# Attention and a GELU feed-forward on one core: how the first GEMM of a batch is opened

## The chip, the cores and the metric

The kernel runs on one core of a Trainium2 chip. The time is the device time of one execution in microseconds; the median of three runs stands for a kernel. A separate execution was recorded by the hardware profiler; its rows name engines: PE is TensorE (matmuls), DVE is VectorE, ACT is ScalarE, POOL is GpSimd, SP is the engine that issues most DMAs.

## The reference

Eight batches of eight heads, 576 tokens, head dimension 64; then a feed-forward with 512 inputs, 2048 hidden units and 512 outputs, on all 4608 tokens.

```python
scores = scale * np.matmul(q, k.transpose(0, 1, 3, 2))
log_f = np.log(np.clip(f, 0.0001, 1.0))
cum = np.cumsum(log_f, axis=-1)
decay = cum[:, :, :, None] - cum[:, :, None, :]
scores = np.where(causal, -1000000000.0, scores + decay)
attn = softmax(scores)
x = (attn @ v), heads side by side, (B * S, H * D)
h = x @ w_in
out = gelu(h) @ w_out          # exact GELU, with erf
```

## The kernel before

**Batches and stages.** The loop at the end runs over the eight batches. For batches 2 to 7 `attention(b)` (line 828) does the attention of batch b and opens its first GEMM; the loop behind it finishes that GEMM. The second GEMM of batch b - 1 is not a stage of its own: `gemm2_rows` (line 489) is a generator, one step at each `yield`, and `take(fill, n)` runs n steps of it wherever the attention of batch b has room. Batches 3 to 7 use `PLAN` (line 472) and the counts in `FILL` (line 825); batch 2 uses other plans.

**The order is written by hand.** Each engine executes its instructions in the order in which the program emits them, and so does each DMA queue. Waits between engines are semaphores that the framework places from the reads and writes of the tiles.

**Scores.** The heads are taken in four pairs, i = 0 to 3. For each pair `scores` (line 299) makes four tiles, t = 0 to 3: matmuls on 64 rows into a tile of two PSUM banks (tag `s`, two such tiles in all), an exp on ScalarE from PSUM into SBUF, and for the tiles on the diagonal a mask on GpSimd. After tile t of pair i come `FILL[i][t]` steps of the second GEMM. The third tile of any row needs the buffer of the tile two before it, so it waits for that tile's exp.

**The second GEMM's steps.** A row tile of 128 tokens (ts = 0 to 3) has 16 steps, one for each block of 128 hidden units. A step "r" is two matmuls on 64 rows each, into two banks; a step "n" is one matmul on 128 rows into the first bank. After the last "r" VectorE copies the second bank to `ot`, and after the last step it adds the first (line 533) and SP stores the tile. Row tiles 0 and 2 hold the two banks of tag `o`, 1 and 3 those of tag `m`. In row tiles 0 to 2 all 16 steps are "r", and the two banks change their parts at the end, so that the bank allocated first is copied first. For row tile 3 the copy is put off (line 521) until `put_off.pop()()` (line 867), after AV.

**AV.** For a pair, `av(i, n)` makes the two heads' products: `attend` (line 343) is 15 matmuls of 65 columns into one bank of tag `o`, `normalize` (line 358) a reciprocal and a multiply on VectorE from that bank into `x`. n steps of the second GEMM stand between the two heads. Then `x_dma` (line 388) transposes the pair's part of `x` into `xT` by a DMA that SP issues. There are two `o` banks, so a head waits for the normalisation of the head two before it, and the first two heads wait for what empties row tile 2's banks.

**The first GEMM.** `gemm1(c, ffb, kts, ps, act)` (line 400) computes block ffb of 128 hidden units (16 blocks), with four matmuls of 512 columns; number kt needs the x transpose of pair kt. `gelu` on ScalarE takes the bank to SBUF. Before, batches 3 to 7 open four blocks in the four `s` banks: kt 0 and 1 of blocks 0 and 1; kt 2 of the same; kt 0 to 2 of blocks 2 and 3; kt 3 of all four; then the four gelus; then block 4 in an `m` bank. The loop goes on with block 5; blocks 6 and 7 lie in `o` banks (`spare`, line 416), the others alternate between the two `m` banks.

**Beside it.** While the first GEMM runs, VectorE unpacks q and k of the next batch (`untangle`, line 260), GpSimd weighs its v (`weigh_v`, line 283), copies the last 64 tokens into `tails` (`x_tail`, line 394) and issues the loads of q and k two batches ahead. SP issues the transposes of q and k, the loads of v, the stores of the output, and the x transposes, all in one queue. The 64 last tokens of every batch go through both GEMMs after batch 7.

Of the kernel before, what the change touches and what calls it, by code (L numbers as in the profile page):

```python
# [9 lines left out]
FP32 = mybir.dt.float32  # L10
# [5 lines left out]
P = 128  # L16
# [3 lines left out]
HP = 4  # L20
# [34 lines left out]
def kernel(  # L55
# [35 lines left out]
    s_psum = ctx.enter_context(tc.tile_pool(name="s_psum", bufs=2, space=PSUM))  # L91
# [153 lines left out]
    def transpose_dma(b, h0, h1):  # L245

        if b >= B:
            return
        if b not in tq_of:
            tq_of[b] = [  # L250
                tq_pool.tile([P, H, JT // 2, PT], BF16, tag="t" + n, name=f"t{n}{b}")
                for n in "qk"
            ]
        for src, dst in zip(qk_of[b], tq_of[b]):
            nc.sync.dma_start_transpose(
                dst[:, h0:h1].rearrange("d h j p -> d (h j) p"),
                src[:, h0:h1].rearrange("p h c -> p (h c)"),
            )
# [84 lines left out]
    def attend(b, i, h, ms, pool=o_psum, tag="o"):  # L343
        if (b, i, h) not in o_of:
            o_of[b, i, h] = pool.tile([P, NBLK, D + 1], FP32, tag=tag, name="o")
        o = o_of[b, i, h]
        for m in ms:
            for n in range(m + 1):
                t, c = where(n, m)
                nc.tensor.matmul(  # L350
                    o[:, m, :],
                    e_of[b, i, t][:, h, c : c + P],
                    vw_of[b][:, 2 * i + h, n, :],
                    start=(n == 0),
                    stop=(n == m),
                )

    def normalize(b, i, h):
        if (b, i) not in x_of:
            x_of[b, i] = x_pool.tile([P, NBLK, 2, D], BF16, tag="x", name="x")  # L360
        o = o_of[b, i, h]
        r = x_pool.tile([P, NBLK], FP32, tag="r", name="r")
        nc.vector.reciprocal(r, o[:, :, D])  # L363
        nc.vector.tensor_tensor(  # L364
            x_of[b, i][:, :, h, :],
            o[:, :, 0:D],
            r.unsqueeze(2).to_broadcast([P, NBLK, D]),
            Alu.mult,
        )

    def xT(b):
        if b not in xT_of:
            xT_of[b] = xT_pool.tile([P, n_dm, XC], BF16, tag="xT", name="xT")
        return xT_of[b]
# [13 lines left out]
    def x_dma(b, i):  # L388
        nc.sync.dma_start_transpose(
            xT(b)[:, i, :].rearrange("d (m p) -> d m p", p=P),  # L390
            x_of[b, i].rearrange("p m h d -> p (m h d)"),
        )
# [7 lines left out]
    def gemm1(c, ffb, kts=range(4), ps=None, act=True):  # L400
        src = xT(c) if c < B else tails
        if ps is None:
            ps = m_psum.tile([P, TC], FP32, tag="m", name="ps1")
        for kt in kts:
            nc.tensor.matmul(  # L405
                ps,
                w_in_sb[:, kt, ffb * P : (ffb + 1) * P],
                src[:, kt, 0:TC],
                start=(kt == 0),
                stop=(kt == n_dm - 1),  # L410
            )
        if n_dm - 1 in kts and act:
            gelu(c, ffb, ps)
        return ps

    def spare():
        return o_psum.tile([P, TC], FP32, tag="o", name="ps1")

    def gelu(c, ffb, ps):
        if c not in g_of:  # L420
            g_of[c] = [
                g_pool.tile([P, TC], BF16, tag=f"g{n}", name=f"g{n}")
                for n in range(n_ff)
            ]
        nc.scalar.activation(g_of[c][ffb], ps, Act.Gelu)  # L425
# [9 lines left out]
    def gemm2(c):  # L435
# [37 lines left out]
        (0, "o", 16 * "r"),  # L473
        (1, "m", 16 * "r"),
        (2, "o", 16 * "r"),
        (3, "m", 4 * "r" + 12 * "n"),
    ]

    PLAN_0 = [(2, "o", 16 * "r"), (3, "m", 14 * "r" + 2 * "n")]
# [105 lines left out]
    def gemm2_third():  # L585
        yield from gemm2_second(0)
        yield from gemm2_rows(0, PLAN_0)
        yield from gemm2_rows(1, PLAN_1)

    def take(gen, n):  # L590
        for _ in range(n):
            if next(gen, "end") == "end":
                return
# [228 lines left out]

    FILL = [[7, 4, 3, 3], [3, 3, 3, 3], [3, 3, 3, 3], [3, 3, 3, 2]]
    FILL_2 = [[8, 8, 8, 8], [8, 8, 4, 4], [4, 4, 4, 4], [4, 4, 4, 4]]

    def attention(b):


        fill = gemm2_third() if b == 2 else gemm2_rows(b - 1, PLAN)
        counts = FILL_2 if b == 2 else FILL

        def av(i, n=0):
            for h in range(2):
                attend(b, i, h, (0, 1, 2, 3, 4))
                normalize(b, i, h)
                if h == 0:
                    take(fill, n)
            x_dma(b, i)  # L840

        for i in range(HP):
            for t in range(4):
                scores(b, i, t)
                take(fill, counts[i][t])
                if t == 1 and b == 2 and i > 0:
                    av(i - 1)
                    if i == 1:
                        load_v(3)
                if b == 2 and (i, t) == (0, 3):  # L850
                    weigh_v(b, 2)
                    weigh_v(b, 3)
                if b > 2 and i == 0 and t == 1:
                    load_v(b + 1)
                if b > 2 and t == 0 and i < 2:
                    transpose_dma(b + 1, 4 * i, 4 * i + 4)
                if b == 2 and t == 1 and i == 1:
                    transpose_dma(3, 0, 4)
        if b == 2:
            take(fill, 4)  # L860
            av(HP - 1)
        else:
            av(0)
            for i in range(1, HP):
                take(fill, 1)
                av(i, 1)
            put_off.pop()()
        take(fill, 4)
        if b == 2:
            transpose_dma(3, 4, 8)  # L870
        take(fill, 999)

        if b == 2:
            pss = [gemm1(b, ffb, (0, 1)) for ffb in range(2)]
            pss += [spare(), spare()]
        else:
            pss = []
            for _ in range(2):
                wide = s_psum.tile([P, 2, 512], FP32, tag="s", name="ps1")
                pss += [wide[:, 0, :], wide[:, 1, :]]  # L880
            for ffb in range(2):
                gemm1(b, ffb, (0, 1), pss[ffb])
        for ffb in range(2):
            gemm1(b, ffb, (2,), pss[ffb])
        for ffb in (2, 3):
            gemm1(b, ffb, (0, 1, 2), pss[ffb])
        for ffb in range(4):
            gemm1(b, ffb, (3,), pss[ffb], b == 2)
        for ffb in range(0 if b == 2 else 4):
            gelu(b, ffb, pss[ffb])  # L890
        if b == 2:
            more = s_psum.tile([P, 2, 512], FP32, tag="s", name="ps1")
            gemm1(b, 4, ps=more[:, 0, :])
        else:
            gemm1(b, 4)
        if b + 1 < B:
            untangle(b + 1, 0)
            weigh_v(b + 1, 0)
        x_tail(b)
# [64 lines left out]
    for b in range(B):  # L964
        if b == 0:
            first_attention()
        elif b == 1:
            second_attention()
        else:
            attention(b)  # L970
        for ffb in range(4 if b < 2 else 5, n_ff):
            if b == 0 and ffb in HELD:
                continue
            aside = ffb in ((7, 8) if b == 2 else (6, 7)) if b > 1 else b == 1 and ffb % 4 < 2
            gemm1(b, ffb, ps=spare() if aside else None)
            if b == 1 and ffb % 2 == 0:
                at = HELD[(ffb - 4) // 2]
                gelu(0, at, h_of[at])
            if b == 0:
                if ffb == 4:  # L980
                    attend_tail()
                if ffb == 5:
                    tail_0()
                if ffb == 7:
                    weigh_v(1, 0)
                    load_w_out(0)
                    weigh_v(1, 1)
                    load_w_out(1)
                    load_qk_tokens(2)
                if ffb == 8:  # L990
                    transposes_first(1, 0, o_psum, "o")
            elif b + 1 < B:
                first, gap = (5, 3) if b == 1 else (1, 4)
                at, late = divmod(ffb - first, gap)
                if late == 0:
                    untangle(b + 1, at)
                if late == gap - 2 and (b > 1 or at < 2):
                    weigh_v(b + 1, at)
                if ffb == (9 if b == 1 else 14):
                    load_qk_tokens(b + 2)  # L1000
# [34 lines left out]
```

## Time and profile before

| what | value |
|---|---|
| median of 3 runs | 340.0 us (339.42 to 340.82) |
| the profiled execution | 340.29 us |
| its span | 338.6 us, 8109 instructions |
| TensorE busy | 322.1 us (95%) |
| ScalarE busy | 205.6 us (61%) |
| VectorE busy | 189.3 us (56%) |
| granted TensorE clock, batches 3 to 7 | 1.00 |
| batches 3 to 7, first score matmul to the next | 36.1, 36.8, 35.7, 35.9, 36.3 us |

A row of a timeline has its start and length in us, the engine, the line of the kernel, the operation, output and inputs, the tile sizes, a count of instructions that were merged, and in brackets the idle time before it with what ended it. Matmuls are pipelined: the bar of one is longer than the distance between two starts. "64*128" is a matmul on 64 rows, "128*128" on 128. A few per cent of the matmul records are missing. Of a group of merged rows the name is that of the first.

### The profile page before, as it was taken

To read this page: it belongs to the slowest core of one execution; us is meant where nothing else is said; L and a number is where in the kernel's file an instruction comes from. 1 tells how busy PE (TensorE), PEld (TensorE's weight loads), DVE (VectorE), ACT (ScalarE), POOL (GpSimd) and SP (SyncE) were. 2 spreads that over 40 slices of the span, in tenths; PEclk is the share of its full clock that TensorE was granted. 3 is DMA by queue.
4 is the path that set the end of the run, shared out by engine and by line. 5 is a ranking of instruction groups with operands and counts; after the bars stand their busy time and mean duration, and the time that the engine had idled before them with its cause. 6 is when DMAs were issued, how large, how long until landed. Compare 5 with 4: busy or idle time off the path is not lost.

```text
span 338.6 us, 8109 instructions
## 1 busy us (share of the span) xinstructions
PE 322.1 (95%) x3284; PEld 174.3 (51%) x3322; DVE 189.3 (56%) x432; ACT 205.6 (61%) x296; POOL 134.2 (40%) x260
## 2 busy tenths in 40 slices
PE   8999999999999998999989999999999989999995
PEld 4654555445544556446634564456545564444443
DVE  5843765755469538963898259934994280020011
ACT  4986867954707991689347962798088916404600
POOL 8987871076354251715261535434252500000000
PEclk9999999999999999999999999999999999999999
DMA  7999999959989695499929983979500151011012
GB/s 116 202 195 214 214 195 132 211 113 202 204 203 181 124 216 129 83 137 223 161 58 159 215 154 95 138 153 223 110 1 2 64 91 50 0 69 57 0 48 79
DMA packets 94949, 44.19 MB, mean 131 GB/s; under 512 B 74176, under 2 KB 89792, under 8 KB 94912
## 3 DMA queue, kind: packets, MB, share of 16 engines
q1 hardware_dynamic: 77760, 27.16, 41.7%
q0 software_dynamic: 16752, 15.99, 29.8%
q8 instruction: 26, 0.43, 0.6%
q10 hardware_dynamic: 400, 0.52, 0.4%
q14 instruction: 11, 0.09, 0.1%
HBM read 36.85 MB, written 9.44 MB: 137 GB/s over the span
## 4 chain that ended last, share of the span: by engine, by line
PE 79%; DMA 7%; ACT 5%; DVE 3%; POOL 3%; issue 2%; POOLq 0%; ACTq 0%; DVEq 0%
PE ps L405 35%; PE ps L509 20%; PE ps L449 8%; PE o L350 7%; PE s L319 6%; DMA xT<-x 5%; ACT L329 2%; ACT e L329 2%; DVE x L364 2%; DMA v_sb<-in_v_dram 2%; ACT g L425 1%; PE ps L573 1%; DVE r L363 1%; PE ps L549 1%; POOL k L120 1%
## 5 line engine op out<-in xcount | busy, mean ns | idle before, releaser
L425 ACT ACTIVATE g<-ps 128x512 bf16<-128x512 f32 x138 | 78.4, 602 | 92.8 <-remote 47.0
L405 PE MATMUL ps<-xT,w_in_sb 128*128 128x512 bf16 x494 | 112.7, 379 | 4.5 <-DMA xT<-x 3.5
L509 PE MATMUL ps<-w_out_sb,g 64*128 64x512 bf16 (+1 forms) x732 | 106.7, 376 | 0.5 <-issue 0.5
L329 ACT ACTIVATE e<-s 128x896 bf16<-128x896 f32 x112 | 87.8, 836 | 14.2 <-PE s L319 9.8
L405 PEld LDWEIGHTS <-w_in_sb 128*128 128x128 bf16 x576 | 55.2, 97 | 70.8 <-issue 7.3
L331 POOL TENSOR_SCALAR_AFFINE_SELECT e<-e 128x256 bf16<-128x256 bf16 (+1 forms) x135 | 49.1, 384 | 79.4 <-ACT e L329 79.0
L509 PEld LDWEIGHTS <-g 64*128 64x128 bf16 (+1 forms) x746 | 42.5, 94 | 28.7 <-issue 1.3
L288 POOL TENSOR_TENSOR vw<-v_sb,wT 128x640 bf16<-128x640 f32 (+1 forms) x30 | 38.3, 1276 | 38.1 <-PE o L350 17.1
L269 DVE COPY qT<-tq 64x288 bf16<-64x288 bf16 x96 | 45.0, 469 | 3.0 <-DMA tq<-q 1.5
L523 DVE COPY ot<-ps 128x512 f32<-128x512 f32 x20 | 13.8, 692 | 56.6 <-PE ps L509 56.6
L269 DVE COPY kT<-tk 64x288 bf16<-64x288 bf16 x96 | 37.9, 395 | 3.9 <-DMA tk<-k 2.2
L319 PE MATMUL s<-qT,kT 64*128 64x256 bf16 (+1 forms) x336 | 37.8, 275 | 1.9 <-DVE kT L241 0.6
L350 PE MATMUL o<-vw,e 128*128 128x65 bf16 x840 | 34.5, 194 | 2.5 <-DVE r L363 1.5
L350 PEld LDWEIGHTS <-e 128*128 128x128 bf16 x840 | 31.0, 97 | 10.1 <-issue 7.0
L458 DVE COPY ot<-ps 128x512 f32<-128x512 f32 (+2 forms) x9 | 5.7, 632 | 50.5 <-PE ps L449 50.5
L319 PEld LDWEIGHTS <-kT 64*128 64x128 bf16 x336 | 18.1, 94 | 20.9 <-issue 6.0
L364 DVE TENSOR_TENSOR x<-o,r 128x320 bf16<-128x320 f32 x56 | 27.5, 491 | 1.9
L449 PE MATMUL ps<-w_out_sb,g 128*128 128x512 bf16 (+2 forms) x142 | 27.9, 355 | 0.2
L449 PEld LDWEIGHTS <-g 128*128 128x128 bf16 x144 | 13.5, 98 | 14.5
L533 DVE TENSOR_TENSOR ot<-ot,ps 128x512 f32<-128x512 f32 x27 | 18.6, 687 | 2.5
L405 PE MATMUL ps<-tails,w_in_sb 128*128 128x512 bf16 x63 | 14.2, 377 | 0.1
L363 DVE RECIPROCAL r<-o 128x5 f32<-128x5 f32 x56 | 10.7, 191 | 4.9 <-PE o L350 3.0
(90 smaller groups left out, 185.8 us busy)
## 6 DMA issues: line engine op xcount, KB each, us to landing
out_dram<-ot SPq DMA_DIRECT2D x32, 256.0 KB, 2.3
v_sb<-in_v_dram SPq DMA_DIRECT2D x24, 256.0 KB, 4.7
q<-in_q_dram POOLq DMA_DIRECT2D x6, 576.0 KB, 6.4
k<-in_k_dram POOLq DMA_DIRECT2D x6, 576.0 KB, 8.6
v_sb<-in_v_dram POOLq DMA_DIRECT2D x17, 128.0 KB, 5.7
w_in_sb<-in_moe_w_in_dram POOLq DMA_DIRECT2D x4, 512.0 KB, 7.8
w_out_sb<-in_moe_w_out_dram POOLq DMA_DIRECT2D x4, 512.0 KB, 8.1
v_sb<-in_v_dram SPq DMA_DIRECT2D x6, 128.0 KB, 4.7
```

The source lines that it names most:

```text
L269: nc.vector.tensor_copy(rows[:, odd], src[odd * D : (odd + 1) * D, 2 * i + h].rearrange("d j p -> d p j"),)
L288: eng.tensor_tensor(vw(b)[:, hs, n0:n1, 0:D], v_sb[:, hs, n0:n1, :], w.unsqueeze(3).to_broadcast([P, 2, n1 - n0, D]), Alu.mult,)
L319: nc.tensor.matmul(to, *ab, start=half < 0, stop=half == 1 or not masked)
L329: nc.scalar.activation(et[:, :, z:c], st[:, :, z:c], Act.Exp, scale=scale)
L331: nc.gpsimd.affine_select(out=et[:, :, c0 + z : c0 + P], in_=et[:, :, c0 + z : c0 + P], compare_op=Alu.is_ge, fill=0.0, base=z, pattern=[[ ...
L350: nc.tensor.matmul(o[:, m, :], e_of[b, i, t][:, h, c : c + P], vw_of[b][:, 2 * i + h, n, :], start=(n == 0), stop=(n == m),)
L364: nc.vector.tensor_tensor(x_of[b, i][:, :, h, :], o[:, :, 0:D], r.unsqueeze(2).to_broadcast([P, NBLK, D]), Alu.mult,)
L405: nc.tensor.matmul(ps, w_in_sb[:, kt, ffb * P : (ffb + 1) * P], src[:, kt, 0:TC], start=(kt == 0), stop=(kt == n_dm - 1),)
L425: nc.scalar.activation(g_of[c][ffb], ps, Act.Gelu)
L449: nc.tensor.matmul(pss[ts][:, c0:c1], g_of[c][kt][:, ts * P : (ts + 1) * P], w_out_sb[:, kt, c0:c1], start=(kt == 0), stop=(kt == n_ff - 1),)
L509: nc.tensor.matmul(banks[r], g_of[c][kt][rows, ts * P : (ts + 1) * P], w_out_sb[rows, kt, :], start=kt == (steps.index("r") if r else 0), ...
L533: nc.vector.tensor_tensor(ot, ot, bank, Alu.add)
```

## The change

For batches 3 to 7 alone:

- Row tile 3 of the second GEMM has two "r" and fourteen "n" steps, where it had four and twelve.
- The steps between score tiles: eight where there were seven after the first tile, and 3, 2, 3, 0 in the last pair where there were 3, 3, 3, 2. In all 50 where there were 52.
- The steps in AV follow `FILL_AV`, pairs of (steps before the pair, steps between its heads): none in pair 0, then 3 and 1, 2 and 1, 2 and 1. Before, it was none, then 1 and 1 for each. In all 10 where there were 6; the last four steps come after AV, where there were six.
- `gemm1_open` opens six blocks, 0 to 3 in the `s` banks, 4 and 5 in the `o` banks: kt 0 and 1 of all six, kt 2 of all six, then kt 3 and the gelus for block 4, block 5, blocks 0 and 1, blocks 2 and 3.
- The loop leaves block 5 out, since it is done; blocks 8 and 9 lie in `o` banks, where it was 6 and 7. Block 6 is the first in an `m` bank.

```diff
-        (3, "m", 4 * "r" + 12 * "n"),
+        (3, "m", 2 * "r" + 14 * "n"),
...
-    FILL = [[7, 4, 3, 3], [3, 3, 3, 3], [3, 3, 3, 3], [3, 3, 3, 2]]
+    FILL = [[8, 4, 3, 3], [3, 3, 3, 3], [3, 3, 3, 3], [3, 2, 3, 0]]
+    FILL_AV = [(0, 0), (3, 1), (2, 1), (2, 1)]
...
+    def gemm1_open(b):
+        pss = []
+        for _ in range(2):
+            wide = s_psum.tile([P, 2, 512], FP32, tag="s", name="ps1")
+            pss += [wide[:, 0, :], wide[:, 1, :]]
+        pss += [spare(), spare()]
+        for ffb in range(6):
+            gemm1(b, ffb, (0, 1), pss[ffb])
+        for ffb in range(6):
+            gemm1(b, ffb, (2,), pss[ffb])
+        for pair in ((4,), (5,), (0, 1), (2, 3)):
+            for ffb in pair:
+                gemm1(b, ffb, (3,), pss[ffb], False)
+            for ffb in pair:
+                gelu(b, ffb, pss[ffb])
...
-            av(0)
-            for i in range(1, HP):
-                take(fill, 1)
-                av(i, 1)
+            for i, (n0, n1) in enumerate(FILL_AV):
+                take(fill, n0)
+                av(i, n1)
             put_off.pop()()
-        take(fill, 4)
         if b == 2:
+            take(fill, 4)
             transpose_dma(3, 4, 8)
         take(fill, 999)
...
-            gemm1(b, 4)
+            gemm1_open(b)
...
-            aside = ffb in ((7, 8) if b == 2 else (6, 7)) if b > 1 else b == 1 and ffb % 4 < 2
-            gemm1(b, ffb, ps=spare() if aside else None)
+            aside = ffb in ((7, 8) if b == 2 else (8, 9)) if b > 1 else b == 1 and ffb % 4 < 2
+            if b <= 2 or ffb > 5:
+                gemm1(b, ffb, ps=spare() if aside else None)
```

More of the change, by code (lines that the diff above doesn't have):

```diff
@@ L875, in attention @@
             pss += [spare(), spare()]
[L876 to L880, printed above, removed]
-            for ffb in range(2):
[L882 to L891, printed above, removed]
+            for ffb in range(2):
+                gemm1(b, ffb, (2,), pss[ffb])
+            for ffb in (2, 3):
+                gemm1(b, ffb, (0, 1, 2), pss[ffb])
+            for ffb in range(4):
+                gemm1(b, ffb, (3,), pss[ffb])
             more = s_psum.tile([P, 2, 512], FP32, tag="s", name="ps1")
```

## The prediction

> **What bounds the kernel now.** I read the page's busy shares first, then TensorE's waits, then the timeline of one middle batch engine by engine, and laid the other four beside it. TensorE is the bound:
>
> ```profile
> PE 322.1 (95%) x3284; PEld 174.3 (51%) x3322; DVE 189.3 (56%) x432; ACT 205.6 (61%) x296; POOL 134.2 (40%) x260
> ```
>
> The change adds and removes no TensorE work to speak of, so only gaps can move. The list of waits says where they are in batches 3 to 7 (columns: total us, times, longest):
>
> ```profile
> PE ps L405 <- DMA xT<-x: 3.5, 5, 1.3
> PE o L350 <- DVE r L363: 1.5, 5, 0.3
> PE o L350 <- DVE x L364: 1.0, 5, 0.2
> ```
>
> These understate the gaps, since a matmul's bar runs on after the next could have started. I count starts instead. Batch 4 on TensorE, from the last steps between scores to the first GEMM (L405):
>
> ```profile
> 161.59 0.61 PE L509 MATMUL ps<-w_out_sb,g 64*128 64x512 bf16 x4
> 162.13 1.26 PE L350 MATMUL o<-vw,e 128*128 128x65 bf16 x30
> 163.68 0.64 PE L350 MATMUL o<-vw,e 128*128 128x65 bf16 x15 [0.30 <-DVE r L363]
> ...
> 165.22 0.64 PE L350 MATMUL o<-vw,e 128*128 128x65 bf16 x15
> 165.69 0.38 PE L509 MATMUL ps<-w_out_sb,g 128*128 128x512 bf16 x1
> 165.91 0.64 PE L350 MATMUL o<-vw,e 128*128 128x65 bf16 x15
> 166.76 0.63 PE L350 MATMUL o<-vw,e 128*128 128x65 bf16 x15 [0.21 <-DVE x L364]
> ...
> 167.92 1.46 PE L509 MATMUL ps<-w_out_sb,g 128*128 128x512 bf16 x6
> 169.21 1.03 PE L405 MATMUL ps<-xT,w_in_sb 128*128 128x512 bf16 x4
> 171.59 10.73 PE L405 MATMUL ps<-xT,w_in_sb 128*128 128x512 bf16 x48 [1.35 <-DMA xT<-x]
> ```
>
> A full matmul starts every 0.216 us (167.92 to 169.21 is six). A head of AV takes 0.47 (165.22 to 165.69). Two heads and two steps are 1.37, yet heads start 1.54 apart two by two (163.68, 165.22, 166.76): 0.17 of gap each time. From 162.13 to 163.68 stand two heads and one step, 1.16, so 0.39 of gap. AV loses 0.73 per batch. (A step in front of 163.68 and of 166.76 has no record; the program has it.) The first GEMM stops after four matmuls: 169.21 + 4 x 0.216 = 170.08, restart 171.59, 1.51 lost on the third x transpose.
>
> Between the scores there is one more gap:
>
> ```profile
> 149.70 1.03 PE L509 MATMUL ps<-w_out_sb,g 64*128 64x512 bf16 x8
> 150.80 0.37 PE L319 MATMUL s<-qT,kT 64*128 64x448 bf16 x2
> ```
>
> Four steps from 149.70 end at 150.56; the third score tile waits until 150.80 for ScalarE (gelu 147.92, table load, first exp from 149.83, 0.92 long).
>
> **The change, part by part.**
>
> *Two "r" steps become "n".* Twelve half matmuls, six pairs, take 1.46 in a row, so a pair starts every (1.46 - 0.38)/5 = 0.217. Same as a full one: nothing.
>
> *First slot 7 to 8.* The third score tile stays where ScalarE puts it; the eighth step fills 0.22 of the 0.24.
>
> *Fourth score group 3,3,3,2 to 3,2,3,0.* All steps now lie one earlier against the score tiles, so step 48, the last of row tile 2, ends about 0.19 earlier (0.02 is lost to the first exp of that group, which ends just as its buffer is wanted). What step 48 releases matters, because AV's heads need its two banks:
>
> ```profile
> 161.22 0.69 DVE L523 COPY ot<-ps 128x512 f32<-128x512 f32 x1 [3.01 <-PE ps L509]
> 162.01 0.69 DVE L533 TENSOR_TENSOR ot<-ot,ps 128x512 f32<-128x512 f32 x1
> ```
>
> Before, two steps covered this. Now TensorE stands in front of the first two heads: head 1 starts 0.05 after the add, at 162.70 - 0.19 + 0.05 = 162.56.
>
> *Steps inside AV 0,0 / 3,1 / 2,1 / 2,1.* From 162.56: seven heads 3.29 and ten steps 2.16, end 168.01. Two heads with three steps are 1.59, over VectorE's 1.54, so its gaps close. Before, AV ended at 167.92 with 58 steps done; now 168.01 with 60. Gain 2 x 0.216 - 0.09 = 0.34 per batch, 1.7 for five. Ends: 0.15 if step 48 comes no earlier; 0.97 if every gap of AV and scores (0.73 + 0.24) went. I take 0.34, which follows the rows.
>
> *Six blocks opened.* Let E be the end of AV. Before, six steps and four matmuls ran before the third x transpose was wanted (the second already by the second of these four). Now four steps stand in front, then twelve matmuls on the first two transposes, six on the third, six on the fourth. The second is wanted at E + 5 x 0.216, where it was E + 7 x 0.216, the third at 16 and the fourth at 22 matmul times. With E 0.09 later, that is E + 1.17, E + 3.55 and E + 4.84 by the old E. The same transfers in the five batches (E, the start of the row of six steps: 131.90, 167.92, 204.73, 240.37, 276.34): in batch 3 TensorE stopped after one matmul, on the second transfer, until 134.13; in the others after four, until 171.59, 207.23, 243.20, 279.55. Lost before: 0.72, 1.51, 0.34, 0.67, 1.05, in all 4.29. After, with landings where they were: batch 3 134.13 - 133.07 = 1.06; batch 4 0.12; batch 5 0.01; batch 6, whose second transfer is issued at 238.24 and takes 3.6 to land, 0.30; batch 7 nothing (the tails copy behind its fourth transfer starts 281.09, wanted 281.18). In all 1.49: gain 2.8. Ends: 4.3 if no transfer is late; -1.0 if the second is late in all five as in batch 3 (5 x 1.06 = 5.3).
>
> One transfer in each batch is the late one, and it is never the same:
>
> ```profile
> 164.22 6.75 SPq L389 DMA_TRANSPOSE xT<-x  x4
> ```
>
> Undisturbed, an issue takes 1.2 and landing 2.4; in batches 3 to 7 the worst took 4.1, 4.2, 3.4, 3.6, 3.8. Within 2 us after each one's issue starts one packet of the instruction queue (131.87, 168.52, 201.68, 238.94, 276.49). There are 26 of them to some 6,600 TensorE instructions (3284 and 3322), one in 254. At E as many instructions have been issued after the change as before in batch 3, and four fewer per batch after that, so I leave the landings where they are. The Trainium skill, "Runtime: NRT & Kernel Launch", section "Instruction fetch mechanics", says that instructions are refilled in blocks of 16 KB and that crossing a block is mostly hidden. By that rule no transfer would be late for it, and this term would be the 4.3; the trace's coincidence says otherwise, and the sum goes by the trace.
>
> *Gelu order, banks 8 and 9.* With T the first last-k matmul, six come in 1.30, then blocks of 0.863 follow; the next to need a ScalarE release late is block 12 at T + 6.47, on block 10, the eleventh gelu. Before, seven gelus in a row stood thus:
>
> ```profile
> 173.94 3.62 ACT L425 ACTIVATE g<-ps 128x512 bf16<-128x512 f32 x7 [10.05 <-remote]
> ```
>
> (3.62 - 0.60)/6 = 0.50 apart at most, though each lasts 0.60. The first starts about T + 0.41, so the eleventh is free to start at T + 5.4, before its own data (T + 5.81), and frees the bank at T + 6.46. No gap; what hides the burst is this overlap. The skill's "TensorEngine Tiling (Array Packing)", section "PSUM Bottleneck", warns against this: TensorE's gain does not speed up emptying PSUM, which can become the bottleneck and should be shared with VectorE. Six gelus on ScalarE alone is that case. By the row the cost is nothing; the rival below prices the other reading.
>
> *What is queued behind.* SP issues the x transposes after this train for the next batch:
>
> ```profile
> 183.99 1.30 SPq L255 DMA_TRANSPOSE tq<-q  x1
> ...
> 196.69 3.17 SPq L537 DMA_DIRECT2D out_dram<-ot  x2
> 201.03 2.33 SPq L389 DMA_TRANSPOSE xT<-x  x1
> ```
>
> Its start waits for VectorE's unpacking, which does not move; it is through by 197.53. The x transpose, wanted up to 1.9 earlier (batch 4's gain 1.39 + 0.34, and 0.19), comes at 199.1: 1.6 left. GpSimd's tails copy and the q and k loads behind it follow the fourth transfer, unmoved.
>
> **Sum.** 1.7 + 2.8 = 4.5. The profiled execution took 340.3 (span 338.6 and 1.7 around it), giving 335.8; it lies 0.3 above the median, so I say 335.6.
>
> **Rivals.**
> - *The second transfer is the late one.* For: batches 3 and 6 do it already, and two steps of its cover are gone. Against: only two of five. In all five: 340.0 - 1.7 + 1.0 = 339.3. An SP train that outruns its 1.6 of slack would end in the same place.
> - *Gelus 0.60 apart.* The eleventh then ends at T + 0.41 + 11 x 0.602 = 7.03, block 12 waits 0.61, five times 3.1: 338.7. For: the page's mean of 602 ns. Against: the row above.
> - *Slower.* Same place, if reading six banks while TensorE fills the others stretches gelus to the 704 ns of a 128x640 exp: 0.46 + 11 x 0.704 = 8.21, block 12 waits 1.74, 8.7 in all, 344.3. It decides from 0.63 per gelu on (0.9 gained per batch). Against: the same row, in which four banks were read while others filled.
> - *No late transfer*: 340.0 - 1.7 - 4.3 = 334.0. For: the packets can fall elsewhere. Against: each of the five batches had one.
>
> **Numbers.** Forecast with its own range 333.8 to 337.0, which takes in the last rival: 0.72. Second transfer late in most batches, 337 to 339.3: 0.15. Gelus 0.60 apart: 0.05. Slower: 0.08. A measurement tells about 0.5% (1.7 us) from no change, so faster means under 338.3: 0.72 and half of the second case, 0.79; same 0.13; slower 0.08. The range 333.8 to 338.2 leaves out some 2 in 10.
>
> **What would show it.** AV heads with no VectorE gap from the third on, but one of about 0.3 in front of each of the first two; the x-transpose waits at 1.5 in all, and those on the second transfer; no gap after 150.80's tile; no wait of L405 on ScalarE. Wrong if L405 waits on gelus, if the late transfer falls on the second in most batches, or if the first two heads wait well over 0.6 together.

## The result, and the profile after

The changed kernel takes 335.97 us in the median of six runs (335.55 to 340.65). Against the kernel before on the same chip it is 0.988 of the time, 95% interval 0.9858 to 0.9901: 1.2% faster, some 4 us. The forecast was 335.6 in 333.8 to 338.2.

The execution that was profiled first had lost 4.9 us before batch 3, in batches that the change does not touch: its first score matmul of batch 3 starts at 116.67 instead of 111.74. Where that time went is not followed here. So below I use a second profile of the same kernel (336.74 in the median of ten runs; ratio 0.989, interval 0.9852 to 0.9928). For comparing traces I use the *section*: from the first score matmul of batch 3 to the last matmul of the kernel. It was 222.55 us before; it is 217.97 in the first profile and 218.21 in the second. The change saves 4.6 and 4.3 us there; the sum in the prediction was 4.5.

The waits of TensorE in the second profile, answering to those of before:

```profile
PE ps L405 <- DMA xT<-x: 1.0, 2, 0.8
PE o L350 <- DVE ot L523: 1.0, 5, 0.2
PE o L350 <- DVE ot L533: 0.8, 5, 0.2
```

The waits of AV on the reciprocal and the multiply (L363, L364) are gone. In their place stand waits on the copy and the add of row tile 2 (L523, L533). The wait for the x transposes has shrunk from 3.5 to 1.0, and no wait of L405 for ScalarE has come in.

Batch 4 on TensorE, from the last steps between scores to the first GEMM, second profile of the changed kernel:

```profile
161.74 0.61 PE L509 MATMUL ps<-w_out_sb,g 64*128 64x512 bf16 x4
162.17 0.32 PE L319 MATMUL s<-qT,kT 64*128 64x320 bf16 x2
162.68 0.63 PE L350 MATMUL o<-vw,e 128*128 128x65 bf16 x15 [0.19 <-DVE ot L523]
163.47 0.63 PE L350 MATMUL o<-vw,e 128*128 128x65 bf16 x15 [0.16 <-DVE ot L533]
163.94 0.81 PE L509 MATMUL ps<-w_out_sb,g 128*128 128x512 bf16 x3
164.59 0.64 PE L350 MATMUL o<-vw,e 128*128 128x65 bf16 x15
...
166.88 0.64 PE L350 MATMUL o<-vw,e 128*128 128x65 bf16 x15
167.36 0.59 PE L509 MATMUL ps<-w_out_sb,g 128*128 128x512 bf16 x2
167.79 0.64 PE L350 MATMUL o<-vw,e 128*128 128x65 bf16 x15
168.26 0.38 PE L509 MATMUL ps<-w_out_sb,g 128*128 128x512 bf16 x1
168.48 0.64 PE L350 MATMUL o<-vw,e 128*128 128x65 bf16 x15
168.95 1.02 PE L509 MATMUL ps<-w_out_sb,g 128*128 128x512 bf16 x4
169.81 4.47 PE L405 MATMUL ps<-xT,w_in_sb 128*128 128x512 bf16 x19
```

From 163.94 on every head and every step follows the one before without a gap: a head 0.47, a step 0.216. The first two heads wait. The first GEMM starts at 169.81 and shows no gap in this merged row; by the starts of its matmuls a pause of 0.21 is hidden in it, in front of the thirteenth matmul, where the third transpose is wanted (it starts at 172.61).

The gap between the score tiles has closed too (same profile; the first eight steps run from 148.94 to 150.67, where the second tile starts):

```profile
150.83 1.03 PE L509 MATMUL ps<-w_out_sb,g 64*128 64x512 bf16 x8
151.72 0.36 PE L319 MATMUL s<-qT,kT 64*128 64x448 bf16 x2
```

Four steps of 0.216 from 150.83 end at 151.69; the third tile starts 0.03 later, where it was 0.24.

### The profile page after: what moved, and what is told of

It reads as the page before. It is cut to its first block, busy times and chain, and to the rows that moved or that the text cites. A ratio compares the mean times of both kernels' runs of the same rounds, so it can differ in the third digit from the quotient of the medians.

```text
span 338.9 us, 8087 instructions
## 1 busy us (share of the span) xinstructions
PE 325.7 (96%) x3274; PEld 177.4 (52%) x3312; DVE 189.8 (56%) x432; ACT 203.9 (60%) x296; POOL 134.0 (40%) x260
## 4 chain that ended last, share of the span: by engine, by line
PE 89%; DMA 4%; DVE 3%; issue 1%; ACT 1%; POOL 0%; DVEq 0%; ACTq 0%; POOLq 0%
PE ps L405 36%; PE ps L509 25%; PE ps L449 8%; PE o L350 7%; PE s L319 6%; DMA xT<-x 3%; PE s L623 2%; PE ps_f L226 1%; DMA q<-in_k_dram 1%; DVE ot L533 1%; DVE ot L523 1%; PE ps L573 1%; PE o L654 1%; PE ps L549 1%; ACT e L329 0%
## 5 line engine op out<-in xcount | busy, mean ns | idle before, releaser
L425 ACT ACTIVATE g<-ps 128x512 bf16<-128x512 f32 x138 | 76.9, 610 | 90.2 <-PE ps L405 89.5
L405 PE MATMUL ps<-xT,w_in_sb 128*128 128x512 bf16 x499 | 113.3, 379 | 2.5 <-DMA xT<-x 1.0
L405 PEld LDWEIGHTS <-w_in_sb 128*128 128x128 bf16 x576 | 55.4, 98 | 68.1 <-issue 4.1
L509 PEld LDWEIGHTS <-g 64*128 64x128 bf16 (+1 forms) x736 | 41.3, 94 | 27.0 <-issue 1.3
L523 DVE COPY ot<-ps 128x512 f32<-128x512 f32 x20 | 13.8, 692 | 52.5 <-PE ps L509 52.5
L269 DVE COPY qT<-tq 64x288 bf16<-64x288 bf16 x96 | 41.4, 431 | 1.5
L269 DVE COPY kT<-tk 64x288 bf16<-64x288 bf16 x96 | 41.0, 427 | 1.7
L350 PEld LDWEIGHTS <-e 128*128 128x128 bf16 x840 | 32.2, 98 | 10.5 <-issue 4.9
L319 PEld LDWEIGHTS <-kT 64*128 64x128 bf16 x336 | 18.8, 94 | 20.5 <-issue 4.0
L364 DVE TENSOR_TENSOR x<-o,r 128x320 bf16<-128x320 f32 x56 | 27.5, 492 | 1.9
L533 DVE TENSOR_TENSOR ot<-ot,ps 128x512 f32<-128x512 f32 x27 | 18.6, 688 | 2.5
L628 ACT ACTIVATE e<-s 128x1024 bf16<-128x1024 f32 (+1 forms) x13 | 12.4, 989 | 5.5 <-PE s L623 5.4
L363 DVE RECIPROCAL r<-o 128x5 f32<-128x5 f32 x56 | 10.8, 192 | 6.3 <-PE o L350 5.9
```

What stands on the lines that cost most here:

```text
L269: nc.vector.tensor_copy(rows[:, odd], src[odd * D : (odd + 1) * D, 2 * i + h].rearrange("d j p -> d p j"),)
L319: nc.tensor.matmul(to, *ab, start=half < 0, stop=half == 1 or not masked)
L350: nc.tensor.matmul(o[:, m, :], e_of[b, i, t][:, h, c : c + P], vw_of[b][:, 2 * i + h, n, :], start=(n == 0), stop=(n == m),)
L364: nc.vector.tensor_tensor(x_of[b, i][:, :, h, :], o[:, :, 0:D], r.unsqueeze(2).to_broadcast([P, NBLK, D]), Alu.mult,)
L405: nc.tensor.matmul(ps, w_in_sb[:, kt, ffb * P : (ffb + 1) * P], src[:, kt, 0:TC], start=(kt == 0), stop=(kt == n_dm - 1),)
L509: nc.tensor.matmul(banks[r], g_of[c][kt][rows, ts * P : (ts + 1) * P], w_out_sb[rows, kt, :], start=kt == (steps.index("r") if r else 0), ...
```

## The experiments

### The changed kernel again

No edit.

> The changed kernel once more, unaltered, beside the others on one chip. Theory A (the gain is AV's closed VectorE gaps, about 1.7 us, and the shorter waits for the x transposes, about 2.8 us; the waits that are left come from one transpose per batch that is late because a block of instructions is fetched beside it): 335.5 to 336.5, the late transposes are the same ones in each batch as in the first profile of this kernel (second, third, first, second, third in batches 3 to 7), waits for them 1.0 to 1.6 us in all. Rival R (which transpose is late is chance, from transfers of other queues): the same time within 1 us, but other transposes late.

Measured: 336.74, ratio 0.989 (0.9852 to 0.9928). That is 0.24 over the stated range, on a chip where the kernel before took 340.79. The late transposes are the second, third, first, second and third in batches 3 to 7, as in the first profile of this kernel and as in the profile of before. The waits, counted from starts of matmuls, are 0.96 in batch 3, 0.21 in batch 4 and 0.37 in batch 7, 1.5 in all (1.3 in the first profile: 0.83 and 0.46 in batches 3 and 4). The latest ones are the same again in the profiles of the next four experiments. Which transpose is late is not chance; rival R, as it is put here, falls.

### Only the opening with six blocks

```diff
-        (3, "m", 2 * "r" + 14 * "n"),
+        (3, "m", 4 * "r" + 12 * "n"),
...
-    FILL = [[8, 4, 3, 3], [3, 3, 3, 3], [3, 3, 3, 3], [3, 2, 3, 0]]
-    FILL_AV = [(0, 0), (3, 1), (2, 1), (2, 1)]
+    FILL = [[7, 4, 3, 3], [3, 3, 3, 3], [3, 3, 3, 3], [3, 3, 3, 2]]
+    FILL_AV = [(0, 0), (1, 1), (1, 1), (1, 1)]
```

> Only the opening with six blocks; the steps of the second GEMM stay as they were before. Theory A: six steps still stand in front, so the second x transpose is wanted 7 matmul times after AV, the third 18, the fourth 24; with landings as in the profile of before only batch 3 waits, 0.7 us, instead of 4.3 us in all: 340.2 - 3.6 = 336.6 (335.8 to 337.4). AV keeps its 0.73 us of gaps. Rival S (the steps are what matters, the opening only hides what returns elsewhere): above 338.5.

Measured: 337.82, ratio 0.9924 (0.9887 to 0.9962). The median lies 0.4 above the stated range, while the section is 219.02: 3.5 us under before, against an expected 3.6. So the opening gave what was expected of it. Of the rest, 1.0 in the profile is the length of what comes before batch 3 (112.74 here, 111.74 in the profile of before), which the edit does not touch. Only batch 3 waits for an x transpose, 0.72. In batch 4, where 1.51 were lost, the first GEMM now runs through:

```profile
168.92 1.46 PE L509 MATMUL ps<-w_out_sb,g 128*128 128x512 bf16 x6
170.22 5.15 PE L405 MATMUL ps<-xT,w_in_sb 128*128 128x512 bf16 x23
```

Rival S, over 338.5, falls.

### Only the steps moved

The kernel before with the three lines of the plan and the loop of AV from the change:

```diff
-        (3, "m", 4 * "r" + 12 * "n"),
+        (3, "m", 2 * "r" + 14 * "n"),
...
-    FILL = [[7, 4, 3, 3], [3, 3, 3, 3], [3, 3, 3, 3], [3, 3, 3, 2]]
+    FILL = [[8, 4, 3, 3], [3, 3, 3, 3], [3, 3, 3, 3], [3, 2, 3, 0]]
+    FILL_AV = [(0, 0), (3, 1), (2, 1), (2, 1)]
...
-            av(0)
-            for i in range(1, HP):
-                take(fill, 1)
-                av(i, 1)
+            for i, (n0, n1) in enumerate(FILL_AV):
+                take(fill, n0)
+                av(i, n1)
```

> Only the steps moved; the first GEMM opens with four blocks as before. Theory A: AV gains 0.34 per batch, 1.7 us, but four steps instead of six stand in front of the first GEMM, and the third transpose is wanted 8 matmul times after AV instead of 10: waits of 1.06, 1.85, 0.7, 1.0, 1.4, together 6.0 instead of 4.3 us, so the gain is paid back: 340.2 (339.4 to 341.0), no change. Rival S: the steps give a gain of their own, 338.5 or less.

Measured: 340.20, ratio 0.9984 (0.995 to 1.0018): no change that can be told. Rival S falls. The section is 222.19, 0.4 under before. AV has gained what it gains in the changed kernel, and the first GEMM pays it back: the waits on the x transposes are 1.04, 1.52, 0.33, 0.69 and 1.94, 5.5 in all by the starts (4.7 by the bars), where they were 4.3. Batch 4 of this kernel:

```profile
167.92 1.02 PE L509 MATMUL ps<-w_out_sb,g 128*128 128x512 bf16 x4
168.78 1.03 PE L405 MATMUL ps<-xT,w_in_sb 128*128 128x512 bf16 x4
171.17 4.04 PE L405 MATMUL ps<-xT,w_in_sb 128*128 128x512 bf16 x18 [1.36 <-DMA xT<-x]
```

So the steps are worth something only beside the opening. 3.5 for the one and 0.4 for the other make 3.9 of the 4.3 to 4.6 of both; the rest fits the part of AV's gain that the opening stops the transposes from taking back; no run shows that part by itself.

### Six blocks opened by k

```diff
-        for ffb in range(6):
-            gemm1(b, ffb, (0, 1), pss[ffb])
-        for ffb in range(6):
-            gemm1(b, ffb, (2,), pss[ffb])
+        for kt in range(3):
+            for ffb in range(6):
+                gemm1(b, ffb, (kt,), pss[ffb])
```

> The changed kernel, but the six blocks are opened by k: all six with the first x transpose, then all six with the second, then the third. Theory A: the second is wanted 10 matmul times after AV instead of 5, which is later than it landed in any batch (at most 2.3 us after AV; wanted 2.25), the third and fourth as in the changed kernel: the wait of 0.8 us in batch 3 goes, those on the third stay (0.1 to 0.5 in one batch): 335.2, 0.6 to 1.0 us under the changed kernel on this chip. Rival Q (the wait only moves on to the next transpose, since SP issues them in a row): the same time as the changed kernel within 0.3 us.

Measured: 335.57, ratio 0.9862 (0.9813 to 0.9912); the interval overlaps that of the changed kernel, so the times alone do not part the theories. The traces do. The section is 217.36, 0.6 to 0.9 under the changed kernel's. In batch 3 the second transpose is as late as ever (it lands 1.94 after AV; 2.00 in the second profile of the changed kernel), and TensorE does not notice:

```profile
132.43 1.02 PE L509 MATMUL ps<-w_out_sb,g 128*128 128x512 bf16 x4
133.29 5.99 PE L405 MATMUL ps<-xT,w_in_sb 128*128 128x512 bf16 x27
```

The waits on the third stay, 0.43 in batch 4 and 0.24 in batch 7. Rival Q, the wait that moves on, falls. (The expectation's own figures, landed "at most 2.3" and wanted at 2.25, do not make its "later". The want is 10 x 0.216 = 2.16 after AV, and the second transpose landed 2.00 after AV at the latest in the two profiles of the changed kernel.)

### Two steps into the waits of the first heads

On top of the edit by k:

```diff
-        (3, "m", 2 * "r" + 14 * "n"),
+        (3, "m", 3 * "r" + 13 * "n"),
...
-    FILL = [[8, 4, 3, 3], [3, 3, 3, 3], [3, 3, 3, 3], [3, 2, 3, 0]]
-    FILL_AV = [(0, 0), (3, 1), (2, 1), (2, 1)]
+    FILL = [[8, 4, 3, 3], [3, 3, 3, 3], [3, 3, 3, 3], [3, 2, 3, 1]]
+    FILL_AV = [(0, 1), (2, 1), (2, 1), (2, 1)]
```

> The kernel opened by k, and two of the steps go into the waits in front of the first two AV heads: one after the last score tile (3,2,3,1, so row tile 3 has three r steps), one between head 0 and head 1, while only two stand in front of the third head; three steps are left after AV. Theory A: those two heads wait 0.26 and 0.33 us for the banks of row tile 2 whatever stands there, so two steps of 0.216 are free: AV ends 0.22 us earlier with one more step done, 0.43 us per batch, 2.0 us in all (1.5 to 2.2), 333.6 on a chip where the kernel opened by k takes 335.6. Rival H (the heads wait for something behind TensorE's own progress, so the wait returns behind the steps, or the x transposes, 0.2 us earlier wanted, take it back): less than 0.7 us.

Measured: 333.44, ratio 0.980 (0.9776 to 0.9824). It is faster than the kernel before, and the interval lies clear of the changed kernel's. The execution that was profiled took 338.32; its batch 3 starts only at 116.98. The section is 215.36, 2.0 under that of the kernel opened by k, as expected. The first heads start when they did, 14.01 after the batch's first score matmul in batch 3 (14.00 in the changed kernel); AV ends 0.21 earlier with one more step done (20.06 against 20.27). The wait of the first head on L523 is gone from the list:

```profile
PE o L350 <- DVE ot L533: 0.8, 5, 0.2
```

The x transposes do take back a little, as rival H has it: the first GEMM waits 0.23 in batch 3 on the second transpose, 0.22 in batch 4 on the third and 0.40 in batch 5 on the first, 0.85 in all, where it was 0.67. Batch 5:

```profile
206.11 0.64 PE L350 MATMUL o<-vw,e 128*128 128x65 bf16 x15
206.80 0.59 PE L509 MATMUL ps<-w_out_sb,g 128*128 128x512 bf16 x2
207.63 6.63 PE L405 MATMUL ps<-xT,w_in_sb 128*128 128x512 bf16 x30 [0.24 <-DMA xT<-x]
```

AV ends at 206.11 + 0.47 = 206.58, and three steps (the first has no record) end at 207.23; the first GEMM starts 0.40 later. Five times 0.43 less 0.18, by which these waits have grown, is the 2.0. So the prediction's account of the two waits in front of the heads holds: they hang on VectorE's copy and add behind step 48, not on TensorE's own progress, and two steps fit into them free of charge.

### TensorE's instruction stream shifted by half a block, and by a whole one

```diff
         warm_up(9)
+        warm_up(64, 32)
```

> The changed kernel with 64 more matmuls of 32 columns in the warm-up at the start, where TensorE waits for the first loads; nothing else. It moves all later work 128 instructions on in TensorE's stream, so the instruction blocks are fetched 128 instructions earlier in the work. Theory F (a transpose is late because the fetch of a block of TensorE's instructions runs beside it): the late ones move: batch 3 from the second to the first, batch 4 from the third to the first or second, batch 5 from the first to the second, batch 6 from the second to the fourth or none, batch 7 from the third to the first or second; in each the instruction packet still stands within 2 us after the issue. Rival R (late for a reason that is tied to the transposes' own place, the queue or the other traffic): second, third, first, second, third, as in all profiles so far.

The same with 128 in place of 64:

> As the run with 64 extra matmuls, but with 128 of them: 256 instructions more, as many as one fetched block seems to hold (one fetch in some 254 instructions). Theory F: the fetches fall on the same places of the work as without any, so the late transposes are second, third, first, second, third again, and the waits of the first GEMM come back in batch 3 on the second transpose (0.8 to 1.0 us). Rival G (the extra work at the start only moved the phase of something that runs by time, so that the pattern is arbitrary after any shift): some other pattern.

Both stand on the changed kernel. One execution each, 337.85 and 343.31; these times carry the extra matmuls, and batch 3 starts at 114.70 and 118.87, so only the pattern is read. The table gives the time from issue to landing in us of the four x transposes of each batch (the late ones in bold). Behind them stands how long after the start of the latest one's issue a packet of the instruction queue starts; each of these packets is 16 KB in the trace.

| batch | changed kernel | 128 instructions more | 256 instructions more |
|---|---|---|---|
| 3 | 2.41, **4.20**, 3.07, 2.38; packet at 2.0 | **3.11**, 2.42, 2.39, 2.39; 0.3 | 2.40, **4.07**, 2.93, 2.40; 1.9 |
| 4 | 2.77, 2.38, **4.27**, 3.38; 1.3 | 2.38, **3.58**, 2.65, 2.39; 1.0 | 2.67, 2.38, **4.60**, 3.70; 1.3 |
| 5 | **4.41**, 3.18, 2.46, 2.37; 0.9 | 2.38, 2.38, **3.09**, 2.42; 0.6 | **3.56**, 2.46, 2.36, 2.37; 0.9 |
| 6 | 2.37, **3.11**, 2.41, 2.48; 0.6 | 3.33, 2.39, 2.39, **3.95**; 1.3 | 2.38, **3.38**, 2.42, 2.47; 0.6 |
| 7 | 2.38, 2.37, **4.42**, 3.56; 1.2 | 2.37, **3.30**, 2.41, 2.48; 0.5 | 2.38, 2.37, **4.39**, 3.53; 1.1 |

With 128 instructions more, the late transpose is another one in all five batches. Four are as expected; in batch 5 it is the third, where the second was expected. In batch 6 there are two packets, and two are late; the other packet starts 0.5 before the issue of the first. (In batch 4 of the two other kernels there is a second packet too. It starts 0.6 and 0.9 before the issue of the first, which lands at 2.77 and 2.67.) With 256 more, the first pattern is back, and with it the wait on the second transpose in batch 3, 0.83 by the starts. First the kernel with 128 more, then with 256 more, from the end of AV in batch 3 (of the four steps in the first row one has no record):

```profile
134.97 1.02 PE L509 MATMUL ps<-w_out_sb,g 128*128 128x512 bf16 x3
135.83 4.48 PE L405 MATMUL ps<-xT,w_in_sb 128*128 128x512 bf16 x20
```

```profile
139.15 1.02 PE L509 MATMUL ps<-w_out_sb,g 128*128 128x512 bf16 x4
140.01 0.38 PE L405 MATMUL ps<-xT,w_in_sb 128*128 128x512 bf16 x1
141.06 2.32 PE L405 MATMUL ps<-xT,w_in_sb 128*128 128x512 bf16 x10 [0.67 <-DMA xT<-x]
```

Theory F holds: which transpose is late goes with the place in TensorE's instruction stream, and the packet stands beside it each time. A shift of 128 changes it and one of 256 does not, which fits the one packet to 254 instructions of the prediction. Rivals R and G fall, each by one execution of five batches. What in the DMA makes the two disturb each other stays open.

## Why the prediction was right, point by point

*Sum and time.* The sum of 4.5 stands against 4.3 and 4.6 in the section, and the time of 335.6 against 335.97.

*"r" to "n" at nothing.* Right: after AV four "n" steps take 0.86 (168.95 to 169.81), 0.216 each, as a pair of halves takes.

*Slot 7 to 8 and the AV term, 0.34 per batch.* In batches 4 to 7, AV ended 20.10 after the first score matmul, with 58 steps done; it ends 20.21 after it with 60. That is 0.43 - 0.11 = 0.32. The two new waits were put at about 0.3 each. By the starts of batch 4 in the second profile the first is 0.26: the last score tile ends at 162.31 (it takes 0.14, as 161.45 to 161.59 before), the head starts 0.37 later, and 0.11 of that stood between 64-row and 128-row matmuls before too (161.59 + 2 x 0.216 = 162.02, head at 162.13). The second is 163.47 - 162.68 - 0.47 = 0.32. VectorE's gaps from the third head on closed because three steps with two heads take 1.59, over its 1.54.

*The opening, 1.5 left of 4.29.* Right as a sum: 1.5 and 1.3. Not right batch by batch. Batch 3 was put at 1.06 and shows 0.96 and 0.83; batch 4 at 0.12, and shows 0.21 and 0.46. Batch 6 was put at 0.30 and shows none, because its second transpose lands 0.86 after AV, not 1.42. Batch 7 was put at none and shows 0.37 in one profile and none in the other. The step that was rough is "I leave the landings where they are". The packet does go with the instruction stream, as that passage supposed, so its distance to a transpose shifts with the order of the work: in batch 6 it starts 1.65 before the end of AV, not 1.43, and that transpose took 3.1 instead of 3.6. How much later a transpose lands does not follow from that distance alone: in four other runs (only the opening, opened by k, heads filled, 256 more) the packet starts 0.5 to 0.7 after the issue of the same transpose, and it takes 3.3 to 3.4. Landings that a packet has touched differ by some tenths from one execution to the next (the third of batch 7: 3.71 and 4.42). The prediction also looked for the waits on the second transpose; 0.58 of the 1.5, and 0.46 of the 1.3, fell on the third. That the sum came out is in part luck: what batch 6 did not lose made up for what batches 4 and 7 lost more.

*Instruction fetch.* The Trainium skill, "Runtime: NRT & Kernel Launch", section "Instruction fetch mechanics", gives blocks of 16 KB or 256 instructions; the pattern that returns after 256 agrees. It calls crossing a block mostly hidden. For TensorE's own progress nothing here speaks against that, and the page says nothing of a DMA beside the fetch, so the prediction's "no transfer would be late" is more than it states. Here an x transpose beside a fetch landed 0.7 to 2.2 us later than the undisturbed 2.4, and with the four-block opening TensorE waited in every batch, for the late transpose (batches 3, 4 and 7) or for the third, which had been issued later behind it (batches 5 and 6).

*Gelus at nothing.* Right. The burst in batch 4 of the changed kernel:

```profile
174.32 5.13 ACT L425 ACTIVATE g<-ps 128x512 bf16<-128x512 f32 x10 [9.63 <-PE ps L405]
```

Ten gelus in 5.13: (5.13 - 0.60)/9 = 0.50 apart on average, though each lasts 0.60 (0.48 in the middle of the burst; the tenth starts 0.70 after the ninth, since it has caught up with TensorE). No matmul of L405 waits for ScalarE. The skill's warning about emptying PSUM ("TensorEngine Tiling (Array Packing)", section "PSUM Bottleneck") is about a fourfold gain from array tiling, which the first GEMM here does not have, so "is that case" in the prediction goes too far. At this rate it does not bite; six banks were handed over within 1.3 us and none was missed.

*What is queued behind.* SP starts its first x transpose of a batch 4.02 before AV's end in batches 4 to 7, in the same place in every one, so the train for the next batch did not reach it.

*Rivals.* The second transpose is late in batches 3 and 6 alone, and costs time in batch 3 alone; gelus stay 0.50 apart; so none of the rivals that priced a late second transpose in all batches, gelus 0.60 apart or still slower gelus came about. The rival without any late transpose did not either: each batch has one.

## What to carry to other kernels

Work that is moved to close a gap leaves a hole where it was; look at once which wait it had covered there. Here the steps alone gave nothing (0.9984), because what AV gained the x transposes took, and only more open blocks in front of that wait made it count. When several accumulations are opened on inputs that arrive one by one, open them by input, not by block: the order by k moved the want for the second input back by five matmuls, and the section became 0.6 to 0.9 shorter.

## What was not expected of the hardware

A DMA transpose that has a fetch of TensorE's instructions beside it lands 3.1 to 4.6 us after issue instead of 2.4. Sixty-four matmuls of 32 columns in the warm-up, 128 instructions, moved the late transpose in all five batches, and 128 such matmuls brought the first pattern back.
